# A fused sparse attention and PReLU feed-forward kernel on one core: four start-up steps change engine or place, and one pacing constant changes

## The chip, the core and the metric

The kernel runs on one core of a Trainium2 chip. The metric is device time in microseconds (us) of one execution. Engines are named as in the profile: PE does matmuls, PEld is PE's weight load, DVE, ACT and POOL are the vector, scalar and general engines, SP issues DMAs. POOL and SP each issue DMAs; ACT and DVE issue none here. Line numbers (L177 and so on) are those of the kernel before the change.

## The reference

Eight batches, eight heads, 576 positions, head width 64. Heads 0 to 3 use a local mask (a query sees itself and the 31 positions before it), heads 4 to 7 a strided mask (it sees earlier positions of the same residue modulo 32). What follows is a feed-forward layer on the 4608 tokens, 512 to 2048 to 512, with a learned slope on the negative side.

```python
scores = np.where(mask, q @ k.T / np.sqrt(64), -1e9)     # per batch and head
attn = softmax(scores) @ v
x = attn.transpose(0, 2, 1, 3).reshape(B * S, H * D)      # 4608 x 512
h = x @ w_in                                              # 4608 x 2048
out = (np.maximum(h, 0) + alpha * np.minimum(h, 0)) @ w_out
```

## The kernel before

**Units, pairs and pieces.** A batch is two units: unit 2b holds its local heads, unit 2b+1 its strided heads. Each unit has two pairs of heads, so batch b has pairs 4b to 4b+3 (two local, then two strided). The attention work is a list of small pieces that is written out in program order: transposing q or k of a unit on PE (`transpose_piece`, L221), scores of half a pair (`score_piece` L275 for batches 0 and 1, `score_both` L333 later), probabilities times V (`pv_piece`, L380), and the transposition of a pair's result into the feed-forward's input `xT` (`x_piece`, L410, or a DMA transpose, L424). The feed-forward works on nine chunks of 512 tokens, each with 16 pieces of the first product (`lin1_piece`, L559: four matmuls, a Relu on ACT, a multiply-add on DVE) and 16 of the second (`lin2_piece`, L588: four matmuls).

**Everything is in program order.** All instructions are issued through `keep`, so each engine executes its own instructions in the order in which the source emits them, and the order of pieces is the schedule. `alone` (L458) writes the order for one batch by hand; `attn_step` (L547) emits the next piece. Batch 0 runs alone, with dummy matmuls between the pieces (`warm`, L629). Chunk 0 of the feed-forward then runs with batch 1's pieces between its own. From there the loop at L733 interleaves: in chunk n it spreads the pieces of batch n+1 over the 32 feed-forward pieces by an accumulator, `acc += left / (22.5 - 0.5 * skip) * (0.5 if i < 16 else 1.0)`, where `left` is the number of pieces that remain and i the feed-forward piece. In chunk 6 (n = 6, batch 7, the last one) these are the last attention pieces of the kernel; chunks 7 and 8 have none. Chunk 7's first product reads `xT` of batch 7. Its four matmuls per piece go through the four head pairs in turn; pairs 2 and 3 are batch 7's strided pairs. The last piece of the list transposes pair 31 on PE, is followed by ACT's copy into `xT` (L417), and then by ACT's copy of pair 30 out of a DMA transpose (L435, `x_copy`).

**The start.** SP issues four loads: the constants (identity for PE's transposes, masks; L648), q and k of batch 0's strided heads in float32 (L114), and the slopes. POOL issues the rest: tails, local q and k, V, then the weights, then batch 1. DVE clears buffers, makes `id16` and `madd` from the constants (L681, L682), then casts q to float16 (L684); ACT casts k (L685). PE transposes q, then k. In batches 0 and 1, `transpose_piece` copies each transposed half (e = 0, 1) out of PSUM by a different engine: for q, DVE takes e = 0 and ACT e = 1, for k the other way round (L242 to L248). The two copies of one PSUM tile do not overlap: the second waits for the first through a semaphore (see the order of waits below). `tails` (L253) transposes the last 64 positions and copies them, for q on DVE and for k on ACT. PE's tile for the tails takes the PSUM buffer of q's transposes, and so comes after ACT's copy of q.

**Shared V rows.** Local V is held in 24 windows of 128 rows at a step of 96, so the last 32 rows of a window are the first 32 of the next. In batches 0 and 1 the load brings 96 rows only, and `over_v` (L189) copies the shared 32 rows, 32 x 1495 float16, from partitions 96 to 127 to partitions 0 to 31. `alone` has DVE do this (L463) ahead of the piece `Pv(A[1], 0)`. Probabilities of the local pairs times V need it (first at 21.1 us for batch 0, and at 57.5 us for batch 1).

Of the kernel before, what the change touches and what calls it, by code (L numbers as in the profile page):

```python
# [31 lines left out]
def kernel(  # L32
# [13 lines left out]
    B, H, S, D = q.shape  # L46
# [50 lines left out]
    loaded = {}  # L97
    cast16 = {}

    def load_qk(b, strided, nm):  # L100

        h0 = 4 if strided else 0
        src = q if nm == "q" else k
        if strided and b:
            t16 = hpool.tile([128, 2, 512], F16, tag=f"{nm}s", bufs=3, name=f"{nm}s")
            cast16[(b, True, nm)] = t16
        else:
            t16 = hpool.tile([128, 2, 512], F32, tag=f"{nm}l", bufs=2, name=f"{nm}l")  # L110
            loaded[(b, strided, nm)] = t16
        base = src[b, h0 : h0 + 1, 0:1, :]
        eng = nc.sync if (b > 2 and not strided) or (b == 0 and strided) else nc.gpsimd
        keep(eng.dma_start(t16, bass.AP(  # L114
            tensor=base.tensor, offset=base.offset,
            ap=[[8 * D, 64], [2 * S * D, 2], [S * D, 2], [1, 8 * D]])))
# [12 lines left out]

    def cast_s(b, nm, eng):  # L130
        t16 = hpool.tile([128, 2, 512], F16, tag=f"{nm}s", bufs=3, name=f"{nm}s")
        cast_copy(eng, t16, loaded[(b, True, nm)])
        cast16[(b, True, nm)] = t16

    def cast_l(b, nm, eng="pool"):
        t16 = hpool.tile([128, 8, 2, 64], F16, tag=f"{nm}l16", bufs=2, name=f"{nm}l16")
        cast_copy(eng, t16, loaded[(b, False, nm)].rearrange("p f (t d) -> p t f d", t=8))
        cast16[(b, False, nm)] = t16
# [15 lines left out]
    def load_v(b, strided):  # L154


        if strided:
            st = spool.tile([128, 2048], F16, tag="v", bufs=2, name="stv")
            keep(nc.gpsimd.dma_start(
                st[0:72, :].rearrange("p (h e) -> p h e", h=4),  # L160
                v[b, 4:8, :, :].rearrange("h (p t) d -> p h (t d)", t=8)))
            loaded[b] = st
        else:
            v16 = vls[b % 2]
            base = v[b, 0:1, 0:1, :]
            r0 = 32 if b < 2 else 0
            keep(nc.gpsimd.dma_start(  # L167
                v16[r0:128, :, 0:64],
                bass.AP(tensor=base.tensor, offset=base.offset - (32 - r0) * D,
                        ap=[[D, 128 - r0], [96 * D, 24], [1, D]])))  # L170
            cast16[(b, False, "v")] = v16

    def cast_copy(eng, o, i):
        if eng == "act":
            keep(nc.scalar.copy(o, i))
        elif eng == "dve":
            keep(nc.vector.tensor_copy(o, i))  # L177
        else:
            keep(nc.gpsimd.tensor_copy(o, i))  # L179
# [9 lines left out]
    def over_v(b, eng):  # L189

        v16 = vls[b % 2]
        cast_copy(eng, v16[0:32, 1:24, :], v16[96:128, 0:23, :])
# [28 lines left out]
    def transpose_piece(u, nm):  # L221

        b, strided = u // 2, u % 2 == 1
        early = b < NEARLY
        src = cast16[(b, strided, nm)]
        dst = qTs[u % 2][:, :, 0:576] if nm == "q" else kTs[u % 2][:, :, 32:608]  # L230
        tp = pspool.tile([128, 8, 64, 2], F16, tag="ps", name="tp")
        for j in range(8):
            blk = (src[:, j % 2, 128 * (j // 2) : 128 * (j // 2) + 128] if strided
                   else src[:, j].rearrange("p f d -> p (f d)"))
            keep(nc.tensor.transpose(tp[:, j].rearrange("r p e -> r (p e)"), blk, ident))  # L235
        if strided:
            main = tp.rearrange("r j p e -> r e j p")
            o = dst.rearrange("r e (j p) -> r e j p", j=8)[:, :, :, 0:64]
        else:
            main = tp.rearrange("r t p e -> r e p t")  # L240
            o = dst[:, :, 0:512].rearrange("r e (p t) -> r e p t", t=8)
        if early:  # L242
            for e in range(2):
                eng = "dve" if (nm == "q") == (e == 0) else "act"
                if nm == "k" and e == 1:
                    tails(b, u, strided)
                cast_copy(eng, o[:, e : e + 1], main[:, e : e + 1])
            return  # L248
        cast_copy("dve" if nm == "q" else "act", o, main)
        if nm == "k":  # L250
            tails(b, u, strided)
# [128 lines left out]
    def pv_piece(P, a):  # L380
        while defer and any(P.et[z][0] is defer_et["et"] for z in P.et):
            defer.pop(0)()
        if P.x16 is None:
            if P.xd and P.strided:
                P.x16 = x16s
            else:
                P.x16 = xpool.tile([128, 1024], F16, tag="x16", name="x16")
        v16 = cast16[(P.b, P.strided, "v")]
        grp = P.pgroups[a]
        r = 72 if P.strided else 128  # L390
        pv = pspool.tile([128, 512], F32, tag="ps", name="pv")
        nb = 2 * len(grp)
        for x in range(nb):
            t, hh = grp[x // 2], x % 2
            et, c = P.et[(t, hh)]
            keep(nc.tensor.matmul(  # L396
                pv[:, 65 * x : 65 * x + 65], et[0:r, c : c + 128],
                v16[0:r, 2 * P.pr + hh, t, :] if P.strided else v16[:, 6 * (2 * P.pr + hh) + t, :],
                start=(x == 0), stop=(x == nb - 1), skip_group_check=True))
        w = P.w  # L400
        rc = rpool.tile([128, 8], F32, tag="rc", name="rc")
        pvv = pv[0:w, 0 : 65 * nb].rearrange("r (c e) -> r c e", e=65)
        keep(nc.vector.reciprocal(rc[0:w, 0:nb], pvv[:, :, 64]))  # L403
        c0 = 128 * grp[0]
        keep(nc.vector.tensor_tensor(  # L405
            P.x16[0:w, c0 : c0 + 64 * nb].rearrange("r (c e) -> r c e", e=64),
            pvv[:, :, 0:64],
            rc[0:w, 0:nb].unsqueeze(2).to_broadcast([w, nb, 64]), op=ALU.mult))
# [31 lines left out]
    pairs = [make_pair(g) for g in range(npair)]  # L440
    pieces = []

    def feed(fn, g):
        pieces.append((g, fn))

    def T(u, nm):
        return lambda: transpose_piece(u, nm)

    def Sc(g, i):
        return lambda: score_piece(pairs[g], i)  # L450

    def Pv(g, i):
        return lambda: pv_piece(pairs[g], i)

    def X(g):
        return lambda: x_piece(pairs[g])

    def alone(u0, u1):  # L458

        A, L = (2 * u0, 2 * u0 + 1), (2 * u1, 2 * u1 + 1)  # L460
        fns = [T(u0, "q"), T(u0, "k")] + [Sc(g, i) for g in A for i in range(2)]
        fns += [Pv(A[0], 0), T(u1, "q"), Pv(A[0], 1), T(u1, "k"), Pv(A[0], 2), Sc(L[0], 0), Sc(L[0], 1)]
        fns += [lambda: (over_v(u0 // 2, "dve"), pv_piece(pairs[A[1]], 0)), Sc(L[1], 0), Pv(A[1], 1)]  # L463
        fns += [Sc(L[1], 1), Pv(A[1], 2), Pv(L[0], 0), X(A[0]), Pv(L[0], 1), X(A[1])]
        fns += [Pv(L[1], 0), Pv(L[1], 1), X(L[0]), X(L[1])]
        for fn in fns:
            feed(fn, -1)
# [7 lines left out]
    for g in range(7, npair + 2):  # L475
# [30 lines left out]
        for i, (kind, fn) in enumerate(seq):  # L506
            extra = []
            if todo and i in nslots:
                left = len([z for z in nslots if z >= i])
# [135 lines left out]
    for nm in "qk":  # L645
        keep(nc.vector.memset(qks[nm][64:80], 0.0))
    keep(nc.vector.memset(x16s[64:80], 0.0))
    keep(nc.sync.dma_start(consts, consts_dram))  # L648
    load_qk(0, True, "q")
    load_qk(0, True, "k")  # L650
    keep(nc.sync.dma_start(alpha_r, moe_alpha.rearrange("(kf p) -> kf p", p=128)))
    load_tail(0, True)
# [19 lines left out]
    keep(nc.gpsimd.memset(vls[1][0:32, 0:1, 0:64], 0.0))  # L672
    keep(nc.gpsimd.memset(vls[1][:, :, 64:65], 1.0))
    keep(nc.gpsimd.memset(vss[1][:, :, :, 64:65], 1.0))
    for c in range(4):
        load_w(c, True)
    load_unit(1, True)
# [3 lines left out]
    keep(nc.vector.tensor_copy(id16, ident[0:16, 0:16]))  # L681
    keep(nc.vector.tensor_scalar(  # L682
        madd, consts[:, 128:488], -1.0, 30000.0, op0=ALU.add, op1=ALU.mult))
    cast_s(0, "q", "dve")  # L684
    cast_s(0, "k", "act")  # L685
    apt = pspool.tile([128, 512], F32, tag="ps", name="apt")
    for i in range(end0):
        if i == 1:
# [22 lines left out]
    cast_l(1, "q")  # L711
    load_tail(2, False)
    cast_l(1, "k")
    load_v(2, False)
    load_d(2)
    load_v(2, True)
# [16 lines left out]
    for n in range(1, NCH):  # L733
        ab = attn_until(n + 1) if n + 1 < B else len(pieces)
        left = ab - pos["i"]
        skip = 4 if n == 1 else 0
        acc = 0.0
        for i in range(32):
            if i < 16:
                lin1_piece(n, i)  # L740
            else:
                lin2_piece(n, i - 16)
            if i >= skip:
                acc += left / (22.5 - 0.5 * skip) * (0.5 if i < 16 else 1.0)
            cnt = int(acc)
            acc -= cnt
            attn_n(cnt, ab)
        while pos["i"] < ab:
            attn_step(ab)
# [30 lines left out]
```

The softmax here doesn't subtract the row's maximum and nothing guards it: scores larger than these inputs give would overflow.

## Time and profile before

| what | value |
|---|---|
| median of 7 runs | 323.62 us (323.43 to 323.83) |
| the profiled execution's own time | 323.43 us |
| its span in the trace | 321.7 us |
| PE busy in the first 25.7 us (five stretches) | 3.81 of 5.00, 3.45 of 5.00, 5.00 of 5.00, 4.64 of 5.00, 5.26 of 5.70 us |
| PE busy from 25.7 to 39.5 us (chunk 0, first product) | 13.78 of 13.80 us |
| PE busy from 246.4 to 263.05 us (chunk 6, second product) | 16.02 of 16.65 us |
| DVE, copy of the shared V rows | 17.82 us, 0.54 us long; 52.03 us, 0.97 us long |
| POOL, casts of 128 x 1024 from float32 | 1.03 to 1.37 us |
| load of V's local rows, batch 0 | issued by POOL at 7.12 us, 9.2 us to landing |
| TensorE's granted clock in the slices of the page | 9 of 10 or more throughout |

The span runs from the first to the last instruction of the program; the time of a run has 1.73 us more around it. "Busy" is an engine's own time; a busy PE also counts the dummy matmuls of the start. A row of the timeline gives start and length in us, engine, line and operation, the output and inputs by the program's names with their shapes, how many such instructions are merged in it, and in brackets how long the engine had been idle and what ended the idle time. In the list of waits the numbers are total us, how often, and the longest.

The order of waits on semaphores in the built program, for q of a unit, is: DVE's copy of e = 0 waits for PE, ACT's copy of e = 1 waits for DVE, PE's tail transposes wait for ACT, DVE's copy of q's tails waits for PE, ACT's copy of k's tails waits for DVE.

### The profile page before, as it was taken

To read this page: it belongs to the slowest core of one execution; us is meant where nothing else is said; L and a number is where in the kernel's file an instruction comes from. 1 tells how busy PE (TensorE), PEld (TensorE's weight loads), DVE (VectorE), ACT (ScalarE), POOL (GpSimd) and SP (SyncE) were. 2 spreads that over 40 slices of the span, in tenths; PEclk is the share of its full clock that TensorE was granted. 3 is DMA by queue.
4 is the path that set the end of the run, shared out by engine and by line. 5 is a ranking of instruction groups with operands and counts; after the bars stand their busy time and mean duration, and the time that the engine had idled before them with its cause. 6 is when DMAs were issued, how large, how long until landed. Compare 5 with 4: busy or idle time off the path is not lost.

```text
span 321.7 us, 6320 instructions
## 1 busy us (share of the span) xinstructions
PE 312.4 (97%) x2493; PEld 162.3 (50%) x2493; DVE 182.3 (57%) x356; ACT 172.8 (54%) x321; POOL 141.6 (44%) x152
## 2 busy tenths in 40 slices
PE   7899999999999999999999999999999999999995
PEld 2564455554554454445478654445444544444444
DVE  5576837487545873487338833883387328406801
ACT  2655654468357753774377446754675256416610
POOL 8832398307998446744584348533511300000000
PEclk9999999999999999999999999999999999999999
DMA  7999999995499975997399638972611310020011
GB/s 223 189 206 207 230 206 199 143 264 163 100 153 167 225 75 134 228 123 87 95 186 194 92 101 167 70 94 83 141 29 21 86 65 2 0 98 35 0 65 65
DMA packets 77597, 40.33 MB, mean 125 GB/s; under 512 B 58480, under 2 KB 69248, under 8 KB 77568
## 3 DMA queue, kind: packets, MB, share of 16 engines
q0 software_dynamic: 41728, 17.38, 45.7%
q1 hardware_dynamic: 35840, 22.55, 29.3%
q8 instruction: 19, 0.31, 0.4%
q14 instruction: 10, 0.08, 0.1%
HBM read 38.01 MB, written 9.44 MB: 148 GB/s over the span
## 4 chain that ended last, share of the span: by engine, by line
PE 86%; issue 5%; POOL 2%; DVE 2%; DMA 2%; ACT 2%; SPq 0%; POOLq 0%; ACTq 0%; DVEq 0%
PE ops L610 36%; PE hps L569 35%; PE pv L396 4%; DMA kl<-in_k_dram 2%; PE tp L235 2%; PE sp L353 2%; PE wps L632 1%; PE ops L602 1%; PE xp L413 1%; PE sph L311 1%; PE sp L311 1%; PE sph L353 1%; DVE x L405 1%; PE sp L295 1%; POOL vs L179 1%
## 5 line engine op out<-in xcount | busy, mean ns | idle before, releaser
L582 DVE SCALAR_TENSOR_TENSOR gT<-neg,oma,hps 128x512 f16<-128x512 f32 x144 | 106.2, 744 | 52.6 <-ACT neg L579 44.5
L610 PE MATMUL ops<-wout,gT 128*128 128x512 f16 x560 | 135.3, 379 | 0.0
L569 PE MATMUL hps<-xT,win 128*128 128x512 f16 (+1 forms) x640 | 132.7, 358 | 1.1 <-ACT xT L435 0.6
L579 ACT ACTIVATE neg<-hps 128x512 f32<-128x512 f32 x144 | 86.0, 598 | 38.7 <-PE hps L569 38.7
L569 PEld LDWEIGHTS <-win 128*128 128x128 f16 x640 | 60.2, 98 | 60.3 <-issue 3.9
L610 PEld LDWEIGHTS <-gT 128*128 128x128 f16 x560 | 49.1, 97 | 47.2
L368 POOL TENSOR_TENSOR et<-et,consts 128x576 f16<-128x576 f16 (+1 forms) x24 | 30.6, 1274 | 83.1 <-ACT et L366 83.0
L615 ACT COPY osb<-ops 128x512 f32<-128x512 f32 x35 | 20.5, 586 | 64.8 <-PE ops L610 64.5
L403 DVE RECIPROCAL rc<-pv 72x6 f32<-72x6 f32 (+2 forms) x80 | 14.9, 186 | 53.4 <-PE pv L396 53.0
L405 DVE TENSOR_TENSOR x<-pv,rc 96x384 f16<-96x384 f32 (+2 forms) x62 | 33.0, 532 | 2.1
L396 PEld LDWEIGHTS <-et 72*128 72x128 f16 (+1 forms) x448 | 24.2, 98 | 16.5 <-POOL et L375 0.9
L375 POOL TENSOR_TENSOR et<-et,consts 128x576 f16<-128x576 f16 (+1 forms) x24 | 30.5, 1270 | 2.4 <-ACT et L372 2.4
L366 ACT ACTIVATE et<-sp 128x576 f16<-128x576 f32 (+1 forms) x24 | 15.5, 646 | 11.3 <-PE sp L353 11.3
L372 ACT ACTIVATE et<-sph 128x288 f16<-128x288 f32 (+1 forms) x48 | 18.6, 408 | 0.0
L632 PE MATMUL wps<-wrm 128*128 128x512 f16 x44 | 15.5, 424 | 1.2 <-DVE wrm L644 1.2
L396 PE MATMUL pv<-vs,et 72*128 72x65 f16 x256 | 15.7, 193 | 0.0
L167 POOL DMA_DIRECT2D vl<-in_v_dram x8 | 11.3, 1408 | 7.0 <-PE pv L396 5.9
L179 POOL COPY vs<-stv 72x1024 f16<-72x1024 f16 x14 | 14.3, 1034 | 0.0
L177 DVE COPY qT<-tp 128x1024 f16<-128x1024 f16 (+1 forms) x10 | 10.1, 1009 | 4.0 <-PE tp L235 4.0
L353 PEld LDWEIGHTS <-kT 64*128 64x128 f16 x336 | 7.1, 95 | 9.9 <-issue 8.9
L396 PE MATMUL pv<-vl,et 128*128 128x65 f16 x192 | 10.9, 194 | 0.4 <-POOL et L375 0.4
L417 ACT COPY xT<-xp 128x576 f16<-128x576 f16 x10 | 6.4, 640 | 6.5 <-PE xp L413 6.5
(79 smaller groups left out, 199.2 us busy)
## 6 DMA issues: line engine op xcount, KB each, us to landing
out_dram<-osb SPq DMA_DIRECT2D x35, 256.0 KB, 2.3
ql<-in_q_dram SPq DMA_DIRECT2D x6, 512.0 KB, 5.1
kl<-in_k_dram SPq DMA_DIRECT2D x6, 512.0 KB, 5.9
stv<-in_v_dram POOLq DMA_DIRECT2D x8, 288.0 KB, 6.8
vl<-in_v_dram POOLq DMA_DIRECT2D x6, 384.0 KB, 8.5
win<-in_moe_w_in_dram POOLq DMA_DIRECT2D x4, 512.0 KB, 10.4
wout<-in_moe_w_out_dram POOLq DMA_DIRECT2D x4, 512.0 KB, 17.6
qsd<-in_q_dram POOLq DMA_DIRECT2D x6, 288.0 KB, 6.9
```

The costliest lines, as they stand in the source:

```text
L179: keep(nc.gpsimd.tensor_copy(o, i))
L368: keep(nc.gpsimd.tensor_tensor(mv, mv, m, op=ALU.mult))
L372: keep(nc.scalar.activation(ev[:, n * y : n * y + n], sps[y][0:r, 0:n], AF.Exp, scale=SCALE))
L375: keep(nc.gpsimd.tensor_tensor(mv, mv, m, op=ALU.mult))
L396: keep(nc.tensor.matmul(pv[:, 65 * x : 65 * x + 65], et[0:r, c : c + 128], v16[0:r, 2 * P.pr + hh, t, :] if P.strided else v16[:, 6 * (2 * ...
L405: keep(nc.vector.tensor_tensor(P.x16[0:w, c0 : c0 + 64 * nb].rearrange("r (c e) -> r c e", e=64), pvv[:, :, 0:64], rc[0:w, 0:nb].unsqueeze ...
L569: keep(nc.tensor.matmul(hps[:, dst : dst + w], win16[:, kk, 128 * m : 128 * m + 128], xT[:, kk, src : src + w], start=(kk == 0 and x == 0) ...
L579: keep(nc.scalar.activation(neg, hps, AF.Relu, scale=-1.0))
L582: keep(nc.vector.scalar_tensor_tensor(gTs[n][:, m, :], neg, oma[:, m : m + 1], hps, op0=ALU.mult, op1=ALU.add))
L610: keep(nc.tensor.matmul(ops, gTs[n][:, kf, 128 * mt : 128 * mt + 128], wout16[:, kf, :], start=(kf == 0), stop=(kf == 15)))
L615: keep(nc.scalar.copy(osb, ops))
L632: keep(nc.tensor.matmul(wps, wrm[:, 0:128], wrm, start=True, stop=True))
```

## The change

Five edits, all of them moves or splits of existing work; the computed result is the same.

1. SP issues q of the first strided unit ahead of the constants.
2. The cast of the first strided k is split by halves, the first on DVE (behind its cast of q), the second on ACT.
3. Both copies of the transposed local q of batch 0 (unit 0) are on ACT.
4. The copies of the shared V rows of batches 0 and 1 go from DVE to POOL. For batch 0 POOL does it after its early memsets and the four loads of `w_in`, ahead of the four loads of `w_out` (`load_w(c, True)`). For batch 1 it stands after POOL's cast of batch 1's local k, ahead of the loads for batch 2.
5. In chunk n = 6 the pacing constant is 21 where it was 22.5.

```diff
     def cast_s(b, nm, eng):
         t16 = hpool.tile([128, 2, 512], F16, tag=f"{nm}s", bufs=3, name=f"{nm}s")
-        cast_copy(eng, t16, loaded[(b, True, nm)])
+        if eng[0] == eng[1]:
+            cast_copy(eng[0], t16, loaded[(b, True, nm)])
+        else:
+            for f in range(2):
+                cast_copy(eng[f], t16[:, f : f + 1, :], loaded[(b, True, nm)][:, f : f + 1, :])
...
                 eng = "dve" if (nm == "q") == (e == 0) else "act"
+                if u == 0 and nm == "q":
+                    eng = "act"
...
-        fns += [lambda: (over_v(u0 // 2, "dve"), pv_piece(pairs[A[1]], 0)), Sc(L[1], 0), Pv(A[1], 1)]
+        fns += [Pv(A[1], 0), Sc(L[1], 0), Pv(A[1], 1)]
...
+    load_qk(0, True, "q")
     keep(nc.sync.dma_start(consts, consts_dram))
-    load_qk(0, True, "q")
     load_qk(0, True, "k")
...
     keep(nc.gpsimd.memset(vss[1][:, :, :, 64:65], 1.0))
+    over_v(0, "pool")
     for c in range(4):
         load_w(c, True)
...
-    cast_s(0, "q", "dve")
-    cast_s(0, "k", "act")
+    cast_s(0, "q", ("dve", "dve"))
+    cast_s(0, "k", ("dve", "act"))
...
     cast_l(1, "k")
+    over_v(1, "pool")
     load_v(2, False)
...
-                acc += left / (22.5 - 0.5 * skip) * (0.5 if i < 16 else 1.0)
+                acc += left / ((21 if n == B - 2 else 22.5) - 0.5 * skip) * (0.5 if i < 16 else 1.0)
```

## The prediction, made before the changed kernel ran

> **What bounds the kernel now.** I read the page's busy times first, then the list of PE's waits, then the timeline where each of those waits lies.
>
> The page's first part:
> ```profile
> PE 312.4 (97%) x2493; PEld 162.3 (50%) x2493; DVE 182.3 (57%) x356; ACT 172.8 (54%) x321; POOL 141.6 (44%) x152
> ```
> PE is the bound. The stretches of the windows view show where it is not: from 25.7 us on it is busy nearly throughout (13.78 of 13.80 us in chunk 0's first product), and before that the dummy matmuls make it look busy while a chain of loads, casts and copies sets the pace. So a gain must either shorten that chain, and then everything behind it moves forward, or remove one of the few stalls later. PE's waits:
> ```profile
> PE hps L569 <- ACT xT L435: 0.6, 1, 0.6
> PE tp L235 <- ACT ks L175: 0.5, 1, 0.5
> ...
> PE tt L263 <- ACT qT L175: 0.4, 1, 0.4
> ```
> Each of these three is touched by one edit: the first by the pacing constant, the second by the split of k's cast, the third by moving local q to ACT. No wait on the list names the shared V rows.
>
> **Edits 1 and 2, the first k and the first q.** The timeline of the start:
> ```profile
> 7.34 0.69 DVE L177 COPY qT<-tp 128x512 f16<-128x512 f16 x1 [0.71 <-PE tp L235]
> 7.69 1.04 ACT L175 CAST ks<-kl 128x1024 f16<-128x1024 f32 x1 [5.67 <-DMA kl<-in_k_dram]
> ...
> 8.64 0.58 ACT L175 COPY qT<-tp 128x512 f16<-128x512 f16 x1
> ...
> 8.79 0.62 PE L235 MATMUL tp<-consts,ks 128*128 128x128 f16 x8 [0.47 <-ACT ks L175]
> ...
> 9.34 0.29 PE L258 MATMUL tt<-consts,tl 64*128 64x64 f16 x4
> ```
> k lands at 7.67, ACT casts it whole in 1.04, PE transposes it at 8.79 and the tails at 9.34. Split, DVE's half takes some 0.38 (half of its 0.69 for the same cast of q, and a little more for the start) and ACT's some 0.62, so k could be transposed at 8.34: a hoped-for 0.45. I do not grant it, because of what is queued behind. DVE's half stands ahead of DVE's copy of q (e = 0), which ran at 7.34 while DVE was waiting for nothing else. In the changed order it must wait for k's landing: half of k 7.69 to 8.05, q's copy 8.05 to 8.73. ACT's copy of q (e = 1) waits for DVE's; it can start at 8.75 where it started at 8.64, and ends at 9.34. PE's tail transposes wait for that PSUM buffer: 9.38, where they stood at 9.34. Behind them come DVE's tails of q, ACT's tails of k and the first scores (10.53 before). So the split moves the wait from k's cast to q's copy, and costs 0.04 instead of winning 0.45.
>
> q fetched first issues 0.40 earlier (0.74, where it was 1.14), and the constants land later. Before, the constants took 2.1 from issue to landing (so 2.8), and q 4.8 (so 5.9). [...] The two together landed by 5.91, whichever is first; I put the constants at 5.9. By the rows of before alone (2.1 to landing, issue now ending at 1.9) they would land at 3.7 and cost nothing. [...] So edit 1 is worth 0 by either, as long as the constants land before 6.1; later, each us costs one (landing plus 3.28 is the time of the tails).
>
> **Edit 3, local q of batch 0.**
> ```profile
> 14.74 0.68 DVE L177 COPY qT<-tp 128x512 f16<-128x512 f16 x1
> ...
> 15.46 0.59 ACT L175 COPY qT<-tp 128x512 f16<-128x512 f16 x1 [1.23 <-DVE qT L177]
> ...
> 16.09 0.27 PE L263 MATMUL tt<-consts,tl 128*128 128x128 f16 x2 [0.36 <-ACT qT L175]
> ```
> ACT had been idle for 1.23 when it followed DVE. Alone it starts at 14.74, and its second copy follows 0.48 later (15.46 and 15.94 are two such copies in a row), ending at 15.81 where 16.05 was. PE's tails go to 15.85: 0.24 won. What is late next? ACT's copy of k (e = 0) can start at 15.8 (PE's transposes of k end at 15.74) and end at 16.4; the next scores need it at 16.6 (16.85 less 0.24), so it covers. From there to 25.7 PE's own order sets the pace, and DVE and ACT wait for it, so the 0.24 is carried through.
>
> **Edit 4, shared V rows on POOL.** DVE loses 0.54 at 17.82 and 0.97 at 52.03. Both times it next waited for PE (0.38 and 0.59), so this wins nothing. [...] Zero. [...]
>
> **Edit 5, the pace of chunk 6.**
> ```profile
> 261.16 0.64 ACT L417 COPY xT<-xp 128x576 f16<-128x576 f16 x1 [2.39 <-PE xp L413]
> ...
> 261.69 1.31 ACT L435 COPY xT<-xs 128x576 f16<-128x576 f16 x1
> 261.82 0.59 PE L569 MATMUL hps<-xT,win 128*128 128x512 f16 x2
> ...
> 263.05 7.28 PE L569 MATMUL hps<-xT,win 128*128 128x512 f16 x33 [0.63 <-ACT xT L435]
> ```
> Chunk 7's first two matmuls (local pairs) start at 261.82 and 262.03; the third needs pair 30's copy, which ends at 263.00. It should have started at 262.25 (0.216 each: 13.81 for 64), so 0.80 is lost. The built order after the change has eight second-product matmuls behind the last transposes where there were four, so X, L417 and L435 stand 4 x 0.216 = 0.86 earlier: L435 ends at 262.14, before 262.25. The wait goes entirely, with 0.1 to spare. What moves with it are the score and V pieces of chunk 6, some by four matmuls; their distances to the masks stay two pieces or more. Gain 0.80.
>
> **Sum.** 321.7 - 0.80 - 0.24 + 0.04 = 320.7 of span, with 1.73 around it 322.43. The profiled run (323.43) is 0.19 below the median, so 322.6 for a median.
>
> **Rivals.**
> [...]
> - The split pays in full (0.07), if ACT's copy of q does not hold the tails: 0.45 more, 322.1. Against it is the wait for DVE in both kernels.
> - The pacing does nothing (0.08), if ACT's copies slip behind by over 0.1 or moved pieces stall elsewhere: 0.2 to 0.3 in all, 323.4.
> [...]
>
> **Chances.** Main case 0.55, by itself 322.3 to 322.9. A measurement here tells 0.2% (0.65 us) from no change, so faster means below 322.97: main, the split, and a small part of the first rival, 0.65. Same, to 324.27: the rest of the first rival and the third, with part of the slower case, 0.27. Slower 0.08. The range, 322.2 to 323.4, takes in the first rival and leaves out the last and part of the second.
>
> **What would show it.** Right: no wait of L569 for L435; DVE's q copy near 8.05 and ACT's behind it; first scores within 0.1 of 10.53; tails of local q near 15.85; POOL's copies 1.3 to 3 long with no wait of PE for them; chunk 0's first product at 25.5. Wrong: constants landing after 6.1, first scores at 10.1 or 11, a wait of PE for POOL near 21, or a new wait in chunk 6.

## The result and the profile after

The changed kernel takes 326.13 us (median of 15 runs, 323.84 to 331.15); the kernel before, on the same chip, 323.5 us (35 runs, 323.09 to 324.36). The ratio is 1.0073, with an interval of 1.0058 to 1.0089: slower, and outside the range that was forecast. The profiled execution took 326.46 us with a span of 324.7, 3.0 more than before. Besides the median, the spread has grown, from 1.3 us to 7.3 us; in the 157 further executions of the kernel before that are on record with the experiments, three took over 326 (326.19, 327.4 and 327.7), so long ones are rare there, but not unknown. The medians and ranges here are those of all runs; the ratios leave out runs more than 1.5% above a kernel's quickest, so the long tail that some kernels show is in the ranges, not in the ratios.

Where the 3.0 us lie is read from the same points of the timeline in both profiles (line numbers of the changed kernel are 4 to 8 higher behind its first edit: L177 is L181, L175 is L179, L258 is L264, L681 is L688). All entries are in us; the first row gives points of time, the others distances.

| step | before | after | grown by |
|---|---|---|---|
| k lands | 7.67 | 9.93 | 2.26 |
| k's landing to the tails' transposes | 1.67 | 2.02 | 0.35 |
| tails to the first scores | 1.19 | 1.55 | 0.36 |
| first scores to the first probabilities times V | 3.13 | 4.22 | 1.09 |
| from there to local q's transposes | 0.40 | 0.40 | 0 |
| local q's transposes to its tails | 2.03 | 1.77 | -0.26 |
| its tails to chunk 0's first product | 9.13 | 9.1 | 0 |
| chunk 7's wait for pair 30 | 0.80 | 0 | -0.80 |
| sum | | | 3.0 |

So two of the forecast gains came at their size, and the start lost 4.06 us (the first four rows) that were not in the sum. The first scores and the first product with V before, then the first product with V in the changed kernel (its first scores stand in the timeline below):

```profile
10.53 0.30 PE L295 MATMUL sp<-qT,kT 64*128 64x72 f16 x8
13.66 0.35 PE L396 MATMUL pv<-vs,et 72*128 72x65 f16 x6
```
```profile
17.72 0.35 PE L402 MATMUL pv<-vs,et 72*128 72x65 f16 x6
```

The row of the granted clock on the page before, then the changed page's busy times and its row of the clock:

```profile
PEclk9999999999999999999999999999999999999999
```

```profile
PE 314.4 (97%) x2493; PEld 162.8 (50%) x2493; DVE 181.1 (56%) x354; ACT 173.0 (53%) x322; POOL 143.9 (44%) x154
...
PEclk9799999999999999999999999999999999999999
```

PE has 2.0 us more for the same 2493 matmuls, and the second slice of the clock shows 7 where all were 9: some matmuls ran slower, between 8.1 and 16.2 us (a slice is a fortieth of the span). The timeline of the start, changed kernel (start and length in us, engine, line, operation; in brackets what ended the idle time before it):

```profile
0.74 0.74 SPq L114 DMA_DIRECT2D ql<-in_q_dram  x1
...
1.54 0.58 SPq L655 DMA_DIRECT2D consts<-consts  x1
...
2.17 0.62 SPq L114 DMA_DIRECT2D kl<-in_k_dram  x1
...
5.67 0.36 DVE L688 CAST id<-consts 16x16 f32<-16x16 f16 x1 [1.17 <-DMA consts<-consts]
...
9.36 1.04 POOL L183 CAST ql<-ql 128x1024 f16<-128x1024 f32 x1 [1.52 <-DMA ql<-in_q_dram]
9.95 0.62 ACT L179 CAST ks<-kl 128x512 f16<-128x512 f32 x1 [7.93 <-DMA kl<-in_k_dram]
9.95 0.72 DVE L181 CAST ks<-kl 128x512 f16<-128x512 f32 x1 [2.92 <-DMA kl<-in_k_dram]
...
11.95 0.27 PE L264 MATMUL tt<-consts,tl 64*128 64x64 f16 x4 [0.51 <-ACT qT L179]
...
13.50 0.42 PE L301 MATMUL sp<-qT,kT 64*128 64x72 f16 x8
...
17.29 1.42 POOL L183 COPY vl<-vl 32x1495 f16<-32x1495 f16 x1 [1.88 <-DMA vl<-in_v_dram]
...
18.77 1.07 ACT L179 COPY qT<-tp 128x512 f16<-128x512 f16 x2 [0.49 <-PE tp L239]
...
19.89 0.27 PE L269 MATMUL tt<-consts,tl 128*128 128x128 f16 x2
```

The constants are in by 5.67, as forecast. k, issued only 0.20 later than before, is cast 2.26 later: its own load takes 7.8 from issue to landing where it took 5.7. The list of PE's waits in the first 31 us has a name at its head that was not on the list before:

```profile
PE apt L696 <- DMA alpha_r<-in_moe_alpha_dram: 2.1, 1, 2.1
...
PE tp L239 <- DVE qs L181: 0.8, 1, 0.8
PE tt L264 <- ACT qT L179: 0.5, 1, 0.5
```

The slopes (`alpha_r`) come behind k on SP's queue, and PE needs them just ahead of k; the wait is for the tail of that queue. What came of PE standing still is read from the windows view, which gives the granted clock of each stretch (the column PEclk):

```profile
core 0: us, PE busy (x) PEld busy (x) DVE busy (x) ACT busy (x) POOL busy (x), PEclk, DMA share, GB/s
8.40:10.66 2.26, 0.18 (x2) 0.01 (x1) 0.71 (x2) 0.62 (x1) 1.30 (x2) 1.00 1.28 247
10.66:12.68 2.02, 1.51 (x16) 1.11 (x17) 1.12 (x6) 1.07 (x2) 1.56 (x3) 1.00 1.95 165
12.68:16.09 3.41, 3.41 (x25) 1.08 (x23) 1.59 (x3) 1.38 (x5) 2.73 (x6) 0.50 2.43 132
16.09:20.00 3.91, 3.81 (x57) 2.61 (x56) 1.49 (x4) 2.89 (x8) 2.71 (x3) 1.00 1.24 204
```

PE is busy for 0.18 of 2.26 us while it waits, and soon after its clock is half for 3.41 us, in the stretch that holds the first scores. That stretch is the 1.09 of the table, and part of the 0.36 ahead of it: in it PE is busy throughout with 25 matmuls, where the next stretch, half a us longer, has 57. The stretch of 3.41 before the fall was not idle throughout: counted back from the fall at 12.68 in steps of 3.41, PE was busy for 1.51 us from 9.26 on, and for 1.87 in the step before, after which the clock stayed up. The two other profiles with a fall are alike: PE was busy for 1.06 (e9) and 0.80 us (e14) in the 3.41 before it, and for 1.82 and 2.19 in the step before that. So in these three traces the clock fell after steps with 1.90, 2.35 and 2.61 us of idling, and stayed up after steps with 1.54, 1.59 and 1.22.

In chunk 7 the wait is gone. L441 (L435 before) ends at 265.94, and the first product runs from 265.62 without a break:

```profile
264.63 1.31 ACT L441 COPY xT<-xs 128x576 f16<-128x576 f16 x1
265.62 2.11 PE L575 MATMUL hps<-xT,win 128*128 128x512 f16 x9
```

### The profile page after: what moved, and what is told of

Read it like the earlier page. It is cut to its first block, busy times and chain, and to the rows that moved or that the text cites. A ratio compares the mean times of both kernels' runs of the same rounds, so it can differ in the third digit from the quotient of the medians.

```text
span 324.7 us, 6319 instructions
## 1 busy us (share of the span) xinstructions
PE 314.4 (97%) x2493; PEld 162.8 (50%) x2493; DVE 181.1 (56%) x354; ACT 173.0 (53%) x322; POOL 143.9 (44%) x154
## 4 chain that ended last, share of the span: by engine, by line
PE 90%; DMA 2%; DVE 2%; ACT 2%; POOL 2%; issue 1%; SPq 0%; ACTq 0%; DVEq 0%
PE hps L575 38%; PE ops L616 37%; PE pv L402 4%; DMA kl<-in_k_dram 2%; PE tp L239 2%; PE wps L638 2%; PE sp L359 2%; PE xp L419 1%; PE ops L608 1%; PE sph L317 1%; PE sp L317 1%; PE sph L359 1%; ACT qT L179 1%; PE sp L301 1%; PE sph L301 1%
## 5 line engine op out<-in xcount | busy, mean ns | idle before, releaser
L638 PE MATMUL wps<-wrm 128*128 128x512 f16 x44 | 17.0, 462 | 1.2 <-DVE wrm L650 1.2
L402 PE MATMUL pv<-vs,et 72*128 72x65 f16 x256 | 15.7, 193 | 0.0
L181 DVE COPY qT<-tp 128x1024 f16<-128x1024 f16 (+1 forms) x9 | 9.4, 1044 | 3.3 <-PE tp L239 3.3
L411 DVE TENSOR_TENSOR x16s<-pv,rc 72x384 f16<-72x384 f32 (+1 forms) x18 | 9.2, 509 | 0.6
```

Source lines behind the costliest of these rows:

```text
L402: keep(nc.tensor.matmul(pv[:, 65 * x : 65 * x + 65], et[0:r, c : c + 128], v16[0:r, 2 * P.pr + hh, t, :] if P.strided else v16[:, 6 * (2 * ...
L411: keep(nc.vector.tensor_tensor(P.x16[0:w, c0 : c0 + 64 * nb].rearrange("r (c e) -> r c e", e=64), pvv[:, :, 0:64], rc[0:w, 0:nb].unsqueeze ...
L638: keep(nc.tensor.matmul(wps, wrm[:, 0:128], wrm, start=True, stop=True))
```

## The experiments

Ratios are to the kernel before on the same chip (323.5 to 323.57 us); the start of chunk 0's first product, 25.22 before and 29.0 after, is the common measure of the start. The edits are numbered as in the change. Two theories stood at the beginning: either edit 1 loses the time, by making k late, or the loss comes from the split of k's cast (edit 2) or from POOL's copy (edit 4).

### Which edit it is

**e1_consts_first**: the changed kernel with edit 1 undone.
```diff
-    load_qk(0, True, "q")
     keep(nc.sync.dma_start(consts, consts_dram))
+    load_qk(0, True, "q")
     load_qk(0, True, "k")
```


> The changed kernel with edit 1 undone (constants ahead of q again), edits 2 to 5 kept. Theory A (the order of SP's loads is at fault: with q first, k lands 2.26 us later and PE then stands idle so long that its clock falls to half): k lands near 7.7 us, no stretch at half clock after 6 us, first scores at 10.5 to 10.9, and the time is 0.65 to 1.05 us below the kernel before (ratio 0.9967 to 0.998). Theory B (the split of k's cast or another of edits 2 to 4 is at fault): the start stays 2 us or more behind and the time stays above the kernel before (ratio 1.003 or more).

322.67 us (322.31 to 322.85, 6 runs), ratio 0.9973 (0.9962 to 0.9984). The loss is gone, and so is the spread. k lands at 7.64, and the rest of the start is as forecast:

```profile
7.66 0.43 DVE L181 CAST ks<-kl 128x512 f16<-128x512 f32 x1 [0.64 <-DMA kl<-in_k_dram]
...
8.72 0.58 ACT L179 COPY qT<-tp 128x512 f16<-128x512 f16 x1 [0.44 <-DVE qT L181]
...
9.36 0.27 PE L264 MATMUL tt<-consts,tl 64*128 64x64 f16 x4
```

**e2_q_first**: the kernel before with edit 1 alone (the diff of edit 1).

> The kernel before with edit 1 alone (q ahead of the constants). Theory A: k lands at 9 to 10.5 us instead of 7.7, PE's clock falls to half for about 3.4 us, the time scatters by some us, and its median is 2.6 to 4 us above the kernel before (ratio 1.008 to 1.012). Theory B: k lands near 7.7, DVE's cast of q starts near 6.05, and the time is within 0.2% of before.

325.32 us (323.26 to 331.29, 22 runs), ratio 1.0046 (1.0029 to 1.0063). Edit 1 alone makes the loss and the spread: seven executions lie within 323.26 to 324.21, the others at 325.09 and above. The profile happened to catch one of the seven (323.57 us, k at 7.45), which by itself would have acquitted the edit. So the same kernel was profiled once more:

**e9_q_first_again**: the same kernel, one execution.

> Once more the kernel before with edit 1 alone, one execution, for its trace: the first look caught one of its quickest executions (323.57 us, k landed at 7.45). Theory A1: in an execution near or above its median of 325.3, k's last rows lie behind the start of POOL's 4096-byte rows (6.1 to 6.4 us) at some 0.24 us apiece, k lands after 8.3, and the loss in time up to the first product of chunk 0 follows the landing of k, plus 1 to 1.7 us where the clock falls to half. Against it: a time over 325 with k landed before 7.7.

327.43 us. k lands at 10.12, PE waits 2.0 for the slopes, the clock is half from 11.14 to 14.56, and chunk 0's product comes 3.9 us later than before:

```profile
8.40:11.14 2.74, 0.39 (x2) 0.13 (x1) 0.20 (x2) 1.00 (x2) 1.71 (x2) 1.00 1.37 261
11.14:14.56 3.42, 3.32 (x24) 1.65 (x24) 1.44 (x5) 1.44 (x5) 2.90 (x5) 0.50 2.57 139
```

One kernel, two executions, and k's landing differs by 2.7 us. This is one part of the spread; the clock is the other. Each execution's mean granted clock is on record: of the 22 of e2, sixteen have 0.998 or more and took 323.26 to 326.11, and the six with 0.977 to 0.995 took 325.18 to 331.29.

**e3_pace, e4_k_split, e12_v_rows_pool, e8_local_q_pace**: the kernel before with edit 5, with edit 2, with edit 4, and with edits 3 and 5.

> The kernel before with edit 5 alone (21 in place of 22.5 in chunk 6). Both theories: the wait of chunk 7's third matmul is gone, 0.80 us less (ratio 0.9975), with the start as before (first product of chunk 0 at 25.7 us). A rival: the moved pieces stall elsewhere and the ratio is 0.999 to 1.001.

> The kernel before with edit 2 alone (first k cast by DVE and ACT). Theory A: k lands near 7.7, DVE's half ends near 8.1 and its copy of q near 8.75, ACT's copy of q ends near 9.35, first scores within 0.1 us of 10.53, so the time is 0 to 0.1 us above before; if POOL holds DVE's half, up to 0.6 above (ratio 1.000 to 1.002). Theory B: 2 us or more above (ratio 1.006 or more). The split's own promise would be 0.45 below (ratio 0.9986).

> The kernel before with edit 4 alone (shared V rows by POOL). Expected: POOL's copies start at 16.3 and 48.3 and take 1.3 to 1.6 us, no wait of PE for them, loads for batch 2 issued 2 to 3.4 us later and nothing late, ratio 0.9995 to 1.0005. [...]

> The kernel before with edits 3 and 5 alone: local q of batch 0 on ACT, and the new pace. Expected by the sums: 0.80 + 0.24 = 1.04 us below before, ratio 0.9968, tails of local q 1.77 us behind PE's transposes of it. If moving local q does nothing, 0.80 as in the run with the pace alone (ratio 0.9975).

| run | edits | median us (range, runs) | ratio (interval) |
|---|---|---|---|
| e3_pace | 5 | 322.65 (322.43 to 323.35, 6) | 0.9975 (0.9964 to 0.9986) |
| e4_k_split | 2 | 323.64 (323.35 to 324.5, 13) | 1.0004 (0.9996 to 1.0012) |
| e12_v_rows_pool | 4 | 323.47 (323.12 to 327.75, 13) | 1.0008 (0.9988 to 1.0028) |
| e8_local_q_pace | 3 and 5 | 322.51 (322.04 to 322.75, 22) | 0.9962 (0.9951 to 0.9974) |

The other four edits do what the sum said: pacing gains 0.85; local q's 0.14 beyond it lies within the intervals, so its gain is read from the profiles alone (0.26 in the table of the start, and the same 1.77 for 2.03 in e8's); the split and the shared rows can't be told from nothing. POOL's copy takes 1.42 in each batch, at 15.7 and 48.8, and no wait of PE for it appears.

### What a late k costs, and the clock

**e5_fill**: the changed kernel with ten more dummy matmuls after the transposes of q, so that PE does not idle while k is on its way.
```diff
-            warm(4)
+            warm(14 if i == 0 else 4)
```


> The changed kernel with ten more dummy matmuls behind PE's transposes of the first q (14 for 4), so that PE stays busy while k is late. If the fallen clock is part of the loss (some 1.4 us of the 3.8 that the start lost in the profile): no stretch at half clock after the first 7 us, and the median falls to 1 to 2 us below the changed kernel, ratio to before 0.999 to 1.004, with less scatter. If the clock only accompanies the late k: within 0.5 us of the changed kernel (ratio 1.006 to 1.009). If k lands on time, the dummies themselves cost up to 2 us.

325.08 us (323.87 to 326.2, 22 runs), ratio 1.0044 (1.003 to 1.0058): 1.05 less than the changed kernel, and the runs above 326.2 are gone. In its profile k lands at 9.35, still late, and the clock stays up:

```profile
12.68:16.09 3.41, 3.41 (x52) 1.90 (x52) 1.06 (x3) 2.47 (x6) 2.44 (x6) 1.00 1.88 155
```

The same stretch that held 25 matmuls at half clock holds 52. From first scores to first PV takes 3.13, as before the change. The halved clock is thus worth about 1.1 us of the 4.06, and it is a consequence: the late k is the larger part and stays. In medians, undoing edit 1 (e1) gains 3.46 us on the changed kernel, of which the filled gap gains 1.05 and the other 2.41 are the late k's, less what the extra matmuls themselves may cost.

The clock makes the long executions. Of the changed kernel's 16 on record, the profiled one included, five had a mean clock of 1.000 and took 323.84 to 325.72; the other eleven, at 0.978 to 0.995, took 325.66 to 331.15. All 22 of e5 have 0.998 or more. The slowest, 0.978 over 329.4 us of span, lacks 7.2 us of full clock where one stretch of 3.41 at half lacks 1.7: an estimate of about four such stretches, though no profile caught that execution.

### Why k is late

Three causes were thought of: that a large load at the head of SP's queue slows what follows it; that the constants' 128 short rows, now in the middle of the stream, hold k up; and that k's last rows meet the long rows of POOL's loads of local q and k.

**e7_consts_act**: the changed kernel with the constants issued by ACT, so that SP's queue begins with q and goes on with k.
```diff
+    keep(nc.scalar.dma_start(consts, consts_dram))
...
     load_qk(0, True, "q")
-    keep(nc.sync.dma_start(consts, consts_dram))
     load_qk(0, True, "k")
```


> The changed kernel with the constants issued by ACT ahead of its table load, so that SP issues q, k and the slopes one after the other. If the constants between q and k are what makes k late: k lands at 7 to 7.5 us, no scatter, first scores at 9.9 to 10.5, ratio 0.9955 to 0.998. If a large load that opens SP's queue is at fault (A2): k late and scattered as in the changed kernel, ratio 1.004 or more. By A1: between these, as k's rows end earlier by the 0.6 of the constants' issue: ratio 0.996 to 1.001.

322.51 us (321.66 to 323.24, 22 runs), ratio 0.9962 (0.9949 to 0.9975). k lands at 6.84. In this run a large load at the head of the queue, q's 512 KB, did no harm by itself; it is the constants ahead of k that made it late. This run does not part their rows from their issue: without them k was also issued earlier, at 1.53 for 2.17.

**e10_consts_last**: the changed kernel with SP's order q, k, constants, slopes.

> The changed kernel with SP's order q, k, constants. If the constants' rows in front of k are what pushes k's end into POOL's loads: k lands at 6.8 to 7.3, the constants at 7.3 to 8.5, DVE's cast of q right behind them, and the tails 3.28 us after the constants' landing (10.6 to 11.8), so ratio 1.001 to 1.005. If q at the head of the queue alone makes k late: k after 8.5 here too, ratio above 1.005.

325.3 us (323.72 to 326.37, 10 runs), ratio 1.0048 (1.0033 to 1.0063). k lands at 6.77, but the constants at 7.49, and the tails' transposes come at 10.65: the landing plus 3.16, where the forecast had 3.28 for this term. This trades one lateness for the other. The profile shows the quickest of this kernel's ten executions, with a mean clock of 0.999; eight others had 0.989 to 0.995 and took 325.08 to 326.37. In the profile PE idles for 2.03 us ahead of q's transposes, up to 8.52, and the clock stays up; the trace's clock record has a border of its steps of 3.41 at 7.09, inside this wait, which leaves 0.60 of idling in the one step and 1.43 in the next. The borders lie elsewhere in each profile (9.26, 7.73 and 7.51 in the three with a fall). That the same wait, placed otherwise, made the clock fall in the eight fits, but no profile of them was taken.

**e6_q_first_pool_late**: the kernel before with edit 1, and six small memsets of POOL put ahead of its loads of local q and k.

> The kernel before with edit 1, and POOL's six early memsets moved ahead of its loads of local q and k, so that its 4096-byte rows come 1 us or more later. Theory A1 (k's last rows are slowed because they share the DMA engines with POOL's loads): k lands at 7.4 to 8 us, the scatter is gone (all within 1 us), ratio 0.999 to 1.003, the upper end if V's later landing holds the first probabilities times V. Theory A2 (SP's own queue runs unsteadily when a large load opens it, whatever POOL does): k lands late in most executions, the scatter of several us stays, ratio 1.004 or more.

324.59 us (323.66 to 329.52, 22 runs), ratio 1.0025 (1.001 to 1.0039); k at 8.10. It doesn't decide. POOL issued 0.48 later, but its first long row moved only from about 6.3 to 6.36, since other loads stand ahead of it.

Three more runs were made for this question.

**e14_pool_early**: the kernel before, with SP's order untouched (constants first), and POOL's loads of local q and k ahead of its tails.
```diff
-    load_tail(0, True)
     load_qk(0, False, "q")
     load_qk(0, False, "k")
+    load_tail(0, True)
```


> The kernel before (constants first), with POOL's loads of local q and k ahead of its tails, so that its long rows start about 1.3 us earlier and meet the end of k's load, while SP's order is as before. If the collision is the cause: k lands at 8.5 or later, PE waits, the clock halves in some executions, median 325 to 327 with a spread of several us. If the constants' place is the cause: k lands at 7.5 to 7.9 and the median stays within 0.5 of 323.5. The strided tails land later as well, at 6.5 to 8, still ahead of their use at 9.3.

327.66 us (325.73 to 330.31, 6 runs), ratio 1.0143 (1.0101 to 1.0185). The constants land at 2.77, q at 5.79, as before the change, yet k lands at 9.88. The timeline shows the same picture as the changed kernel's:

```profile
9.90 1.04 ACT L175 CAST ks<-kl 128x1024 f16<-128x1024 f32 x1 [7.88 <-DMA kl<-in_k_dram]
10.24 0.23 PE L689 MATMUL apt<-id,alpha_r 16*128 16x16 f32 x1 [2.16 <-DMA alpha_r<-in_moe_alpha_dram]
...
12.30 1.89 PE L632 MATMUL wps<-wrm 128*128 128x512 f16 x4
```

PE waits for the slopes, then four dummy matmuls take 1.89 where they take 1.04 at full clock. So the collision with POOL's long rows is enough to make k late, with the constants where they always were. The dose is larger than in the changed kernel: the long rows begin at 4.31 instead of 6.09.

**e13_q_first_local_sp**: the kernel before with edit 1, and local q and k of batch 0 issued by SP behind the slopes, so that no long rows of POOL are about. **e15_after_local_sp**: the same in the changed kernel.
```diff
-        eng = nc.sync if (b > 2 and not strided) or (b == 0 and strided) else nc.gpsimd
+        eng = nc.sync if (b > 2 and not strided) or b == 0 else nc.gpsimd
```


> The kernel before with edit 1 (q ahead of the constants), and POOL's loads of batch 0's local q and k go to SP's queue behind the slopes, so that POOL has no long rows to move before k is in. If the collision of SP's k with POOL's long rows is the cause: k lands at 7.0 to 7.6 in the profile, no half clock, the spread between executions falls under 1.5 us (8 with edit 1 alone), median 323.0 to 323.8. If the constants' place in the middle of SP's stream is enough by itself: k lands anywhere from 7.5 to 10, the spread stays at several us, median above 324.5. V is issued some 1.4 earlier by POOL and could collide in its turn; then k lands between the two.

> The changed kernel with POOL's loads of local q and k on SP's queue behind the slopes. If the collision is the cause: the loss of edit 1 goes and edits 3 and 5 show, 322.0 to 322.7 with a spread under 1.5. If not: 324.5 to 326 with a spread of several us, as the changed kernel has it.

e13: 324.85 us (323.88 to 326.13, 9 runs), ratio 1.0035 (1.0012 to 1.0057); k at 7.76. e15: 323.78 us (323.01 to 323.94, 13 runs), ratio 0.9994 (0.9974 to 1.0014); k at 8.33. In both profiles the clock stays up, and the long tail of executions is gone (2.3 and 0.9 us of spread, where edit 1 alone had 8 and the changed kernel 7.3); no execution of either has a mean clock under 0.998. But neither median comes down to what that theory said. e15 gains 2.35 on the changed kernel and is still 1.1 above e1; e13's ratio can't be told from that of edit 1 alone (1.0046), and its executions lie in the range of those of e2 that kept their clock. Other rows of POOL lie beside the end of k in their turn, those of the local tails (512 of 128 bytes, from 6.1 on in e13 and 6.3 in e15), and V's arrival at 14.15 makes PE wait 0.6 for its copy in e15. How much of what is left belongs to these and how much to the constants' place by itself, these runs don't tell.

How the rows met can be counted in the trace's records of single rows (SP's q and k have 512 rows of 2 KB; POOL's local q and k have rows of 4 KB):

| execution | POOL's first long row | rows of q, k started after it | last row of k starts | k lands |
|---|---|---|---|---|
| before | 6.34 | 62 | 7.19 | 7.67 |
| changed | 6.09 | 97 | 9.04 | 9.93 |
| e2, edit 1 alone, quick | 6.28 | 34 | 6.92 | 7.45 |
| e9, the same kernel, late | 6.31 | 80 | 9.39 | 10.12 |
| e14, POOL earlier | 4.31 | 334 | 9.22 | 9.88 |
| e7, constants by ACT | 6.13 | 7 | 6.23 | 6.84 |
| e10, constants last | 6.26 | 0 | 6.08 | 6.77 |

In the changed kernel the last rows of k start at 7.46, 7.69, 7.92, 8.16, 8.40, 8.48, 8.56, 8.80 and 9.04, one at a time: mostly 0.23 to 0.24 apart, though each but the last takes 0.084. Behind each of the first four a long row of POOL starts 0.08 later and takes 0.159, and 0.084 + 0.159 = 0.243: a row of one queue, then a row of the other. Before the change the last ones start at 6.95, 7.03, 7.11, 7.19, which leaves no room for a long row between. In this chain of the changed kernel the two queues thus alternated row by row, as far as the trace's records show.

The same starts show what the count of rows hides. From 7.54 on no other row of k was under way, so the landing at 9.93 waited for one lagging chain of rows (which DMA engine moved it, the trace does not tell). e9 has three such chains, 0.23 to 0.24 apart from 7.5 to 8.5. The quick execution of e2 has a lagging chain as well, but its last rows follow each other every 0.08, up to 6.92. In these traces a late landing is thus one or a few chains of rows that are behind and alternate with long rows, at 0.23 to 0.24 a row.

### A better version

**e11_act_local_q_pace**: the kernel before with edits 3 and 5, the constants issued by ACT, and q, k, slopes on SP.

> Edits 3 and 5 with the constants issued by ACT ahead of its table load and SP issuing q, k, slopes; k's cast whole on ACT, V rows on DVE as before. Expected: k lands near 6.9, ACT casts it to 7.95, tails near 8.6, first scores near 9.8, and 0.5 to 0.8 us less than with edits 3 and 5 alone, ratio 0.9938 to 0.9962. If V's landing (12.1 to 12.8) or the probabilities take over as the limit of the start, only 0.1 to 0.3 less (ratio 0.9955).

322.29 us (322.23 to 322.47, 5 runs), ratio 0.9961 (0.9949 to 0.9973). It beats both kernels, but cannot be told from e7 or e8 at 322.51. Its k landed at 7.43, not at e7's 6.84, and its first scores stood at 10.29 for 10.53; since k landed at 7.35 in e3, where the start is untouched, that is no sure gain of the issue by ACT.

## Why the prediction was wrong

**The step that failed** is in edit 1: "So edit 1 is worth 0 by either, as long as the constants land before 6.1". Its condition held: the constants landed at 5.64 where 5.9 was put, and DVE's cast of q began at 6.05. (The 3.28 of the same sentence, from the constants' landing to the tails, and the 6.1 with it, were estimates of the author's; no run shows 3.28. In e10, where the tails came late behind the constants, it was 3.16.) The value did not follow, since the step asked only what happens to the two loads that change places. k stands behind both on the queue, and its landing at 7.67 was carried over unexamined. In the kernel before, the constants' rows started from 1.68 to 2.40, ahead of all of q's (the first at 2.77), when no other load's rows were under way. Moved behind q they started from 4.1 to 5.1, in the full stream, and took 0.42 us of all 16 engines (the sum of their times, divided by 16), out of the time before POOL's long rows begin. k was also issued 0.20 later. Of the loads the forecast watched the constants alone (a landing after 6.1 was to show it wrong); it was k that came late. What is queued behind a moved step was followed for DVE and ACT, but not for SP's queue.

**The chain**, then, with what is shown and what is not. Edit 1 makes the loss and the scatter: shown by undoing it (e1) and by doing it alone (e2, e9). Its way is k's late landing: shown in e9 and in the changed kernel's profile, and by e7 and e10, where k comes early once no constants lie ahead of it. That k's rows are slowed by POOL's long rows: seen row by row in the changed kernel, and shown as sufficient by e14. That it is all of the lateness in the changed kernel: not shown, since e13 and e15 recover only part of it. That the clock then halves, adds some 1.1 us to the median and makes the long executions: shown by e5 and the clock of each execution. Open is why the same kernel lands k at 7.45 in one execution and at 10.12 in another; POOL's first long row came at 6.28 and 6.31 in these two, so it is not POOL's start. The rows show lagging chains that alternate with long rows in the one, and a chain without them in the other; why a chain lags is not shown.

**The lesson of the size.** Some 0.6 us ahead of k (0.42 of rows and 0.20 of issue) became 2.26 of landing in the profiled execution, where the rows pushed over the edge came at a third of their pace (one every 0.24 for one every 0.08), and 2.26 became 4.06 through the clock and the longer cast of k's half below. The forecast gave a slower kernel 0.08. The loss at the start that its range takes in was put at 0.6 at most, and no run shows that size: the split alone (e4) lost 0.03, and the changed kernel's start 4.06.

**Edit 2.** The forecast was 0.04 of loss, because k's half holds up DVE's copy of q. e4 has 0.03 (landing to first scores 2.89 for 2.86), and e1's lines above show the order forecast: half of k at 7.66, copies of q at 8.00 and 8.72, tails at 9.36 (9.38 forecast). Whether POOL's issuing of V's load would delay DVE was hardly tried: it ended at 7.82 in e1 (8.30 before), so that only 0.16 us of DVE's half (0.43 long) lay beside it. In the changed kernel the half took 0.72, beside POOL's cast at 9.36 to 10.40, and this is most of the 0.35 in the table; in e5 it took 0.82 beside POOL's cast, which ended at 9.91. In both it ended 0.27 to 0.28 after the cast did. In the kernel before, DVE's copy of the shared rows took 0.97 at 52.03, beside POOL's casts (51.53 to 53.89), and 0.54 at 17.82, where no cast of POOL ran. That the cast beside it cost DVE's half this time fits, but was not tried by itself.

**Edit 3** was put at 0.24 and gave 0.26 in the profile: ACT's two copies are one row of 1.07 in the timeline, and the tails follow them. **Edit 4** was put at nothing, and gives nothing; the copies were put at 1.3 to 3, an estimate of the author's whose upper end no run shows, and took 1.42. **Edit 5** was put at 0.80 and gave 0.80 in the profile and 0.85 in e3. Two rivals named for these parts (the split in full, the pacing that does nothing) did not come. The 0.29 by which DVE's half took longer beside POOL's cast (0.72 for 0.43) came because k was late.

## What to carry to other kernels

When a load changes its place on a queue, price it for every transfer behind it, and against the moment when another queue starts on the same engines. Here k landed at 7.67 with the constants at the head of the queue, where no other load's rows were under way, at 9.93 with them in mid-stream, and at 6.84 and 6.77 with none ahead of it (e7, e10). A delay of the first operand can cost more than itself: here 2.26 us of k's landing became 4.06 at the start, some 1.1 of it by the clock that fell after TensorE had idled. And when a change widens the scatter, one profile may show either branch: look at several executions, and at the clock of each, before you read the cause from one.

## What was not expected of the hardware

- The order of three loads set not only the time but its scatter: 323.26 to 331.29 us for one kernel, with k's landing between 7.45 and 10.12.
- A 2 KB row took 0.084, and came only every 0.24 while rows of 4 KB of another queue, 0.159 each, came between. In the changed kernel one such chain of rows held up k's whole load of 512 KB.
- TensorE's clock fell to half for 3.41 us after steps of 3.41 us with 1.51, 1.06 and 0.80 us of work in them (the changed kernel, e9, e14), in the changed kernel 2.0 us after work had resumed; the steps before those, with 1.87, 1.82 and 2.19, were not followed by a fall.
